# Turning k, q and scaled q of an mLSTM cell's second chunk by 128x128 transposes, with new hand-written orders

## The chip, the cores and the metric

One NeuronCore of one Trainium2 chip runs the whole kernel. The metric is device time in microseconds (us) for one execution. Below, PE is TensorE (PEld its weight loads), DVE is VectorE, ACT is ScalarE, POOL is GpSimd and SP is SyncE, which here only issues DMAs.

## The reference: an mLSTM cell, then a feed-forward block

Two blocks run one after the other. The first is a recurrent cell over 768 tokens, for 4 batches and 8 heads of 40 values each:

```python
for t in range(S):
    m_new = np.maximum(f_gate[:, :, t] + m, i_gate[:, :, t])
    f_stab = np.exp(f_gate[:, :, t] + m - m_new)
    i_stab = np.exp(i_gate[:, :, t] - m_new)
    C = f_stab * C + i_stab * outer(vt, kt)      # per batch and head, 40 x 40
    n = f_stab * n + i_stab * kt
    h = C @ qt;  denom = max(abs(n . qt), 1)
    y[:, :, t] = sigmoid(o_gate[:, :, t]) * h / denom
```

The second block takes the 3072 rows of 320 values and computes `leaky_relu(x @ w_in) @ w_out` with slope 0.01, where `w_in` is 320x2048 and `w_out` 2048x320. Everything is wanted in float32, but the two weight matrices arrive as float64.

## The kernel before

**Chunks, steps, groups.** The tokens are cut into six chunks of 128. A *step* is one chunk of one batch, with all 8 heads: steps 0 to 3 are chunk 0, steps 4 to 7 chunk 1, and so on. Inside a chunk the recurrence is done in closed form with matmuls (scores k.q, weights from exponents of gate sums, values, state). The outputs of the four steps of a chunk make one *group* of 512 rows for the feed-forward block. While the feed-forward of group g runs, the cell steps of chunk g+1 are put between its matmuls, and the times below fall into three parts: chunk 0 alone (0 to 38 us, "the front"), group 0 with chunk 1 beside it (38 to 129 us), and groups 1 to 5.

**Who sets the order.** PE, DVE, ACT and POOL run exactly in program order. For the front, that order is the string `ORDER` (line 1104): a list of small actions, each of which issues its instructions on its engines. The ones needed here: `ld`, `lo`, `lw`, `fd`, `ll` issue loads on SP (inputs, output gate, weights); `g`, `ge`, `ug` compute, exponentiate and turn the gates; `ab n` spreads gate sums over the partitions with matmuls (line 464) and `abw n` adds a mask to them on DVE (line 474); `tr s i` and `tc s i` turn k (i=0) or q (i=1) of step s on PE and copy the result on ACT (lines 581, 587); `sc` makes scores on PE, `exp` the weights on ACT (line 491), `scm` multiplies the two on DVE (line 603); `st` and `stc` make and copy the state; `val`, `den`, `gate` and `gp` make values, denominators, gated outputs and their scaling (PE, DVE, DVE, POOL); `x s` and `xc s` turn the outputs into `xT` (lines 879, 892); `vu`, `ps`, `tiles` prepare operands on POOL; `warm n` is n matmuls of the identity into a bank that nobody reads (line 338); and `ff j b0 b1` makes hidden columns j for batches b0 to b1.

**Narrowing.** The float64 weights are turned into float32 in seven passes for each of 12 pieces (lines 262 to 279): the first on ACT, six on DVE. `nw n` issues the next pass for piece n (`nw 0 0` and `nw 0 1` for the halves of piece 0). Pieces 0 to 3 are `w_in`, pieces 4 to 11 are `w_out`. From piece 2 on, the passes are dealt out during group 0 by the tuple `PASSES`.

**Group 0.** Its feed-forward is a list of 30 units. Units 0 and 1 are the last two batches of the first two hidden columns; units 2 to 13 are the rest of the hidden columns (line 910), piece 2 being needed from unit 6 and piece 3 from unit 10; units 14 to 29 are the second matmul (line 946), each a quarter of the sum for one batch: units 14 to 17 need pieces 4 and 5, 18 to 21 pieces 6 and 7, 22 to 25 pieces 8 and 9, and 26 to 29 pieces 10 and 11. `PASSES[i]` passes go ahead of unit i; `fetch` says ahead of which unit weights are loaded; `place` says after which units the parts of chunk 1's steps go, in the order parts 4, plain 4, parts 5, plain 5, parts 6, plain 6, the gates of chunk 2, parts 7, plain 7, and then the four `xT` turns.

**A step of chunk 1.** `ahead(s)` first calls `u_split(s)`: natural k and q (tokens on partitions, 8 heads of 40) are turned with 32 matmuls against a 64x64 piece of the identity, one for each head, each of k and q, and each half u of the tokens. A float32 matmul shows as two instructions, so 64 stand in the profile (line 567). ACT copies the two banks into `kqT` with four copies of 40x512 (line 573). `prep_qs(s)` scales q on POOL (line 520). `u_parts(s)` starts with `split_qs(s)`: the scaled q is turned in the same manner, 16 matmuls (32 instructions, line 553) and two ACT copies (line 555) into the rows of `mixed(s)` that its other halves leave free. Then the scores and the state product follow (tile `sd`, lines 653 and 658), for which DVE multiplies by the weights (line 663). `u_plain(s)` is tile `hN` (line 716), the denominator, and the gated output (line 727, POOL line 705). PSUM has two pools of four banks: `mm` for the feed-forward, `ab` and `warm`; `c` for the cell.

Of the kernel before, what the change touches and what calls it, by code (L numbers as in the profile page):

```python
# [22 lines left out]
def kernel(  # L23
# [26 lines left out]
    nc = tc.nc  # L50
# [89 lines left out]
    def mixed(s):  # L140

        n = s % 2
        return qn[:, 2 * n : 2 * n + 2]
# [9 lines left out]
    def prepare_tiles():  # L153

        for u in range(2):
            nc.gpsimd.tensor_copy(cm2[ts(u, SL)], cmask[ts(u, SL), ts(u, SL)])
        for t in rb_t:
            nc.gpsimd.memset(t[:, :, RL:], 0.0)

# [243 lines left out]

    def natural(s, i):

        t = rb_t[s % NR][:, i]
        return t[:, : H * D].rearrange("p (h d) -> p h d", d=D)
# [107 lines left out]
    def prep_qs(s):  # L515
# [3 lines left out]
        d["qs"] = wk.tile([P, Dm], F32, name="y")[:].rearrange("p (h d) -> p h d", d=D)  # L519
        nc.gpsimd.tensor_tensor(  # L520
            d["qs"], natural(s, 1), gT[c][:, 2, ts(b, H)].unsqueeze(2).to_broadcast([P, H, D]), op=ALU.mult,
# [25 lines left out]

    def split_qs(s):

        tq = [psc.tile([P, H, SL], F32, name=f"tq{u}", tag="c") for u in range(2)]  # L550
        for h in range(H):
            for u, toks, rows in subs(s):
                nc.tensor.matmul(tq[u][rows, h, :], lhsT=st[s]["qs"][toks, h], rhs=ident[toks, toks], start=True, stop=True)  # L553
        for u, toks, rows in subs(s):
            nc.scalar.copy(mixed(s)[rows, u], tq[u][rows])

    def u_split(s):
# [3 lines left out]
        src = (d["k"], natural(s, 1))  # L561
        bank = [psc.tile([P, H, SL], F32, name=f"tk{r}", tag="c") for r in range(2)]
        for h in range(H):
            for i in range(2):
                for u, toks, rows in subs(s):
                    out_rows = rows if i == 0 else slice(SL * u, SL * u + D)
                    nc.tensor.matmul(  # L567
                        bank[u][out_rows, h, :], lhsT=src[i][toks, h, :D], rhs=ident[toks, toks], start=True, stop=True,
                    )
        for i in range(2):  # L570
            for u, toks, rows in subs(s):
                out_rows = rows if i == 0 else slice(SL * u, SL * u + D)
                nc.scalar.copy(d["kqT"][rows, i].rearrange("p (h t) -> p h t", t=SL), bank[u][out_rows])
# [531 lines left out]
warm 2; warm 2; g 0; ld 1; ld 0; ge 0; lo 0; ld 2  # L1105
# [3 lines left out]
st 0; o 0; tc 1 1; exp 0; scm 0; exp 1; stc 0; st 1  # L1109
stc 1; warm 5; warm 1; sc 1; warm 6; scm 1; val 0; ab 2  # L1110
g 1; abw 2; abw 3; tr 2 0; tc 2 0; o 1; tr 2 1; val 1
warm 1; tr 3 0; vu 2; ps 1; ge 1; nw 0 0; den 0; gate 1
gate 0; tc 2 1; vu 3; tiles; tc 3 0; exp 2; o 2; warm 5
sc 2; gp 0; den 1; scm 2; nw 0 1; nw 0 0; nw 0 0; ug 1
warm 2; warm 1; nw 0 0; nw 0 1; x 0; tr 3 1; val 2; nw 0 1
warm 4; st 2; xc 0; tc 3 1; exp 3; gate 2; den 2; sc 3
stc 2; gp 1; scm 3; x 1; gp 2; ps 0; fd 4; nw 0 0
nw 0 0; nw 0 1; st 3; ll 4 1; lw 2; warm 5; val 3; nw 0 1
nw 0 0; xc 1; o 3; gate 3; den 3; nw 0 1; nw 0 1; nw 1
nw 1; stc 3; nw 1; ps 3; nw 1; ll 4 2; lw 3; x 2  # L1120
warm 1; ff 0 0 2; gp 3; ps 2; fd 5; ll 5 1; lw 4; x 3
xc 2; xc 3; lw 5; fd 6; fd 7; nw 1; nw 1; ff 1 0 2
ll 5 2; lw 6; nw 1
# [33 lines left out]
    with tc.manual_schedule(engines={E.PE, E.DVE, E.Activation, E.Pool}):  # L1157
        ffs = first_chunk()
        fetch = {1: (3, 4), 16: (7,), 12: (5, 6)}
        PASSES = (6, 0, 3, 0, 3, 3, 0, 3, 0, 2, 1, 0, 5, 1, 11, 0, 1, 3, 3, 3, 1, 12, 2, 3, 4, 0, 2, 1, 2, 21)  # L1160
        place = (1, 6, 11, 12, 16, 18, 19, 20, 22, 23, 25, 25, 26)
# [173 lines left out]
```

## Time and profile before

| what | value |
|---|---|
| median of 3 runs | 484.6 us (484.34 to 484.87) |
| profiled execution, its own time | 484.43 us |
| its span, first to last instruction | 482.3 us |
| around the span (484.43 - 482.3) | 2.1 us |
| PE busy in the span | 476.0 us, 99% |
| DVE, ACT, POOL busy in the span | 364.7, 196.1, 159.9 us |
| granted TensorE clock, mean | 1.000 |

Busy time says how long an engine had an instruction in it. In the stretch from 38 to 130 us, where the changed code lies, the two engines that matter are both nearly full, so neither the mean over the span nor one engine alone tells what a saved microsecond is worth: the order of each queue must be followed.

### The profile page before, as it was taken

The page shows a single profiled execution, that of the slowest core. Times are in us where ns is not written, and L with a number is a line of the kernel's source. Part 1 is how long each engine was busy: PE and PEld are TensorE (multiplying, and loading weights), DVE is VectorE, ACT ScalarE, POOL GpSimd, SP SyncE. Part 2 cuts the span into 40 slices and gives each one's busy share as a digit, 9 for nine tenths or more (in the row PEclk, how much of TensorE's full clock was granted, in tenths as well). Part 3 has the DMA queues.
Part 4 walks back from the last instruction along what each step waited for, and adds up shares of the span by engine and source line. Part 5 has one row for each costly group of instructions (what it writes and reads, how often), then busy time and mean ns, then how long its engine had stood idle before and what let it go on. Part 6 is the DMA issues. An engine that isn't in the chain of part 4 may idle for free.

```text
span 482.3 us, 12771 instructions
## 1 busy us (share of the span) xinstructions
PE 476.0 (99%) x5093; PEld 375.0 (78%) x5093; DVE 364.7 (76%) x601; ACT 196.1 (41%) x499; POOL 159.9 (33%) x207
## 2 busy tenths in 40 slices
PE   8999999999999999999999999999999999999997
PEld 7998855777655499955569985548998899988996
DVE  4689997989917989877897957889899967335611
ACT  3596774553732332305251212624025642156310
POOL 4146052452602727545641645462310002000020
PEclk9999999999999999999999999999999999999999
DMA  7877679786745577677787867773250030100001
GB/s 139 191 156 194 153 181 240 198 196 149 169 116 117 141 155 193 146 173 189 151 185 155 227 145 179 177 184 114 75 217 29 0 110 1 56 1 1 1 1 54
DMA packets 142698, 63.40 MB, mean 131 GB/s; under 512 B 110832, under 2 KB 130864, under 8 KB 142640
## 3 DMA queue, kind: packets, MB, share of 16 engines
q1 hardware_dynamic: 142256, 62.47, 53.8%
q8 instruction: 40, 0.66, 0.6%
q10 hardware_dynamic: 384, 0.13, 0.1%
q14 instruction: 18, 0.15, 0.1%
HBM read 51.68 MB, written 8.27 MB: 124 GB/s over the span
## 4 chain that ended last, share of the span: by engine, by line
PE 95%; DMA 1%; ACT 1%; DVE 1%; issue 0%; ACTq 0%; SPq 0%
PE po L985 32%; PE ph L910 29%; PE ph L836 8%; PE po L946 7%; PE pe L836 4%; PE pT L746 3%; PE sd L653 3%; PE warm L338 1%; PE sd L658 1%; PE hN L716 1%; PE tk L567 1%; PE tq L553 1%; DMA qn<-in_q_dram 1%; PE pa L676 1%; PE sc L596 1%; ACT w L491 0%
## 5 line engine op out<-in xcount | busy, mean ns | idle before, releaser
L910 PE MATMUL ph<-xT,w_in 64*128 64x512 f32 (+1 forms) x680 | 142.3, 569 | 0.4 <-DVE w_in L279 0.3
L910 PEld LDWEIGHTS ph<-xT,w_in 64*128 64x128 f32 x680 | 69.9, 187 | 61.8 <-issue 58.1
L985 PE MATMUL po<-w_out,acts 128*128 128x160 f32 x640 | 90.2, 300 | 0.0
L985 PEld LDWEIGHTS po<-w_out,acts 128*128 128x128 f32 x640 | 87.4, 190 | 1.9 <-ACT w L491 0.8
L918 ACT ACTIVATE acts<-ph 128x512 f32<-128x512 f32 (+1 forms) x68 | 35.1, 567 | 80.3 <-PE ph L910 80.1
L491 ACT ACTIVATE w<-w,gT 128x64 f32<-128x64 f32 (+1 forms) x192 | 51.7, 347 | 27.2 <-POOL w L483 27.2
L631 POOL TENSOR_TENSOR S<-S,f 40x336 f32<-40x336 f32 x36 | 34.2, 949 | 72.9 <-PE pT L746 50.5
L985 PE MATMUL po<-raw,acts 128*128 128x160 f32 x320 | 45.1, 299 | 0.0
L985 PEld LDWEIGHTS po<-raw,acts 128*128 128x128 f32 x320 | 44.0, 190 | 0.0
L1018 POOL TENSOR_TENSOR y<-y,raw 128x160 f32<-128x160 f32 x10 | 6.3, 634 | 113.4 <-ACT y L1017 113.4
L663 DVE TENSOR_TENSOR qn<-w,sd 64x512 f32<-64x512 f32 x40 | 27.4, 685 | 20.3 <-PE sd L658 14.2
L946 PE MATMUL po<-w_out,acts 128*128 128x320 f32 x128 | 36.6, 437 | 0.0
L483 POOL TENSOR_TENSOR w<-w,i 128x512 f32<-128x512 f32 x20 | 31.8, 1588 | 13.4 <-DVE late L264 13.3
L858 DVE SCALAR_TENSOR_TENSOR acts<-ph,acts 128x512 f32<-128x512 f32 x32 | 20.6, 685 | 20.6 <-ACT acts L856 20.6
L544 DVE TENSOR_TENSOR qn<-kqT,late 64x512 f32<-64x512 f32 x32 | 35.0, 1093 | 1.0
L946 PEld LDWEIGHTS po<-w_out,acts 128*128 128x128 f32 x128 | 23.6, 190 | 9.8 <-issue 0.8
L760 POOL TENSOR_TENSOR xb<-xb,den 128x320 f32<-128x320 f32 x16 | 11.6, 727 | 47.8 <-DVE xb L757 47.8
L856 ACT ACTIVATE acts<-pe 128x512 f32<-128x512 f32 x32 | 17.4, 594 | 19.0 <-PE pe L836 18.9
L653 PEld LDWEIGHTS sd<-kqT 40*64 40x64 f32 x640 | 20.1, 135 | 4.5 <-issue 4.3
L764 DVE STREAM_TRANSPOSE x<-xb 128x512 f32<-128x512 f32 x16 | 17.7, 1106 | 7.7 <-POOL xb L760 7.7
L862 ACT ACTIVATE acts<-acts 128x512 f32<-128x512 f32 x32 | 19.7, 633 | 8.1 <-DVE acts L858 8.1
L985 PE MATMUL po<-raw 128*128 128x160 f32 x160 | 22.8, 300 | 0.0
(166 smaller groups left out, 779.1 us busy)
## 6 DMA issues: line engine op xcount, KB each, us to landing
w<-a_dr SPq DMA_DIRECT2D x40, 128.0 KB, 3.5
rb<-in_k_dram SPq DMA_DIRECT2D x64, 80.0 KB, 3.3
rb<-in_q_dram SPq DMA_DIRECT2D x64, 80.0 KB, 2.6
rb<-in_o_gate_dram SPq DMA_DIRECT2D x64, 80.0 KB, 2.5
xT<-x_dr SPq DMA_DIRECT2D x32, 160.0 KB, 3.2
late<-a_dr SPq DMA_DIRECT2D x32, 128.0 KB, 3.4
x_dr<-x SPq DMA_DIRECT2D x16, 256.0 KB, 3.4
kn<-in_k_dram SPq DMA_DIRECT2D x24, 160.0 KB, 3.5
```

What stands on the lines that cost most here:

```text
L483: nc.gpsimd.tensor_tensor(w, w, cm2.unsqueeze(1).to_broadcast([P, H, SL]), op=ALU.add)
L491: yield nc.scalar.activation(w[:, h, :], w[:, h, :], AF.Exp, bias=gT[c][:, 0, bh : bh + 1], scale=1.0)
L544: nc.vector.tensor_tensor(mixed(s)[rows, 1 - r], d["kqT"][rows, 1].rearrange("p (h t) -> p h t", t=SL), d["ea"][rows], op=ALU.mult,)
L631: nc.gpsimd.tensor_tensor(new, old, g, op=ALU.mult)
L653: nc.tensor.matmul(bank[1 - u][toks, h, :], lhsT=kqT[rows, 0, ts(h, SL)], rhs=kqT[rows, 1, ts(h, SL)], start=True, stop=True,)
L663: nc.vector.tensor_tensor(mixed(s)[toks, u], w[toks], bank[1 - u][toks], op=ALU.mult)
L836: nc.tensor.matmul(ph[r][:], lhsT=parts["w", key][n][part, at : at + P], rhs=xs[key][part, slot, :], start=start and slot == 0, stop=stop ...
L858: nc.vector.scalar_tensor_tensor(fs[r], in0=ph[r][:], scalar=1.0 + EPS, in1=fs[r], op0=ALU.mult, op1=ALU.add,)
L910: nc.tensor.matmul(ph[r][:, cols], lhsT=w_row(r, slot, j), rhs=xT[DP * r : DP * (r + 1), slot, bs, :], start=(slot == 0), stop=(slot == KC ...
L918: nc.scalar.activation(acts[:, f, cols], ph[r][:, cols], AF.Prelu, alpha=0.01)
L946: nc.tensor.matmul(po[n][:], lhsT=acts[:, f, ts(n, P)], rhs=w_out[:, f, :], start=(f == 0), stop=(f == NF - 1),)
L985: nc.tensor.matmul(bank[:], lhsT=left[:, f, :], rhs=right[:, f, :], start=f == 0, stop=f == KH - 1)
```

## The change

1. *Chunk 1's turns.* `u_split` turns k and q with four transposes each, of 128 tokens by two heads of 64 (40 values and 24 of padding): 8 instructions for 64. `split_qs` does the same with the scaled q: 4 for 32. The banks then hold all 128 tokens of a head pair, so `to_halves` copies them out with four ACT copies of 40x256 for each bank: 8 copies for 4 in `u_split`, 4 for 2 in `split_qs`. The scaled q's turn takes one bank for two.
2. *Where q lies.* Natural q of chunk 1 is loaded with a stride of 64 a head; the padding is zeroed by two more POOL memsets in `tiles`. The scaled q goes into slot 0 of `mixed(s)` (tile `qn`) instead of a tile `y`.
3. *`ORDER`.* On PE: one `warm` fewer at the start, four more between `st 0` and `st 1`, one more between `ff 0` and `x 3`; `tr 2 1` goes behind `val 1`; `st 3` ahead of `x 1`; `ff 0 0 2` becomes `ff 0 0 1; ff 0 1 2`. On DVE: `stc 0` ahead of `scm 0`; `abw 3` ahead of `abw 2`; `scm 2` ahead of `den 1`; the fourth pass of `nw 0 1` ahead of `scm 3`; the third of `nw 1` ahead of `stc 3`. On POOL `ps 2` goes ahead of `gp 3`. On SP, the weights of `lw 4` and `lw 6` each go one load earlier.
4. *Group 0.* `place` puts parts 5 after unit 10 (11 before), plain 7 after unit 23 (22) and the third `xT` turn after unit 26 (25). `PASSES` moves single passes by one unit. `fetch` names other units for the late weights.

```diff
--- before.py
+++ after.py
@@ -156,6 +156,7 @@
             nc.gpsimd.tensor_copy(cm2[ts(u, SL)], cmask[ts(u, SL), ts(u, SL)])
         for t in rb_t:
             nc.gpsimd.memset(t[:, :, RL:], 0.0)
+            nc.gpsimd.memset(t[:, 1, : H * DP].rearrange("p (h d) -> p h d", d=DP)[:, :, D:], 0.0)
 
     def prepare_step(n):
 
@@ -401,8 +402,14 @@
             st[s]["o"].rearrange("p (h d) -> p h d", d=D), o_gate[b, :, ts(c, P), :].rearrange("h p d -> p h d"),
         )
 
+    def padded(s):
+
+        return rb_t[s % NR][:, 1, : H * DP].rearrange("p (h d) -> p h d", d=DP)
+
     def natural(s, i):
 
+        if i == 1:
+            return padded(s)[:, :, :D]
         t = rb_t[s % NR][:, i]
         return t[:, : H * D].rearrange("p (h d) -> p h d", d=D)
 
@@ -516,9 +523,8 @@
 
         c, b = divmod(s, B)
         d = st[s]
-        d["qs"] = wk.tile([P, Dm], F32, name="y")[:].rearrange("p (h d) -> p h d", d=D)
         nc.gpsimd.tensor_tensor(
-            d["qs"], natural(s, 1), gT[c][:, 2, ts(b, H)].unsqueeze(2).to_broadcast([P, H, D]), op=ALU.mult,
+            mixed(s)[:, 0, :, :D], natural(s, 1), gT[c][:, 2, ts(b, H)].unsqueeze(2).to_broadcast([P, H, D]), op=ALU.mult,
         )
 
     def prep_o(s):
@@ -545,32 +551,30 @@
                 mixed(s)[rows, 1 - r], d["kqT"][rows, 1].rearrange("p (h t) -> p h t", t=SL), d["ea"][rows], op=ALU.mult,
             )
 
+    def turned(name, src):
+
+        bank = psc.tile([P, PR, P], F32, name=name, tag="c")
+        for j in range(PR):
+            nc.tensor.transpose(bank[:, j, :], src[:, 2 * j : 2 * j + 2, :].rearrange("p h d -> p (h d)"), ident[:])
+        return bank
+
+    def to_halves(s, bank, dst):
+
+        for u, toks, rows in subs(s):
+            by = dst(u, rows).rearrange("p (j e) t -> p j e t", e=2)
+            for e in range(2):
+                nc.scalar.copy(by[:, :, e, :], bank[DP * e : DP * e + D, :, toks])
+
     def split_qs(s):
 
-        tq = [psc.tile([P, H, SL], F32, name=f"tq{u}", tag="c") for u in range(2)]
-        for h in range(H):
-            for u, toks, rows in subs(s):
-                nc.tensor.matmul(tq[u][rows, h, :], lhsT=st[s]["qs"][toks, h], rhs=ident[toks, toks], start=True, stop=True)
-        for u, toks, rows in subs(s):
-            nc.scalar.copy(mixed(s)[rows, u], tq[u][rows])
+        to_halves(s, turned("tq", mixed(s)[:, 0]), lambda u, rows: mixed(s)[rows, u])
 
     def u_split(s):
 
         d = st[s]
         d["kqT"] = cw.tile([P, 2, PR * P], F32, name="kqT")
-        src = (d["k"], natural(s, 1))
-        bank = [psc.tile([P, H, SL], F32, name=f"tk{r}", tag="c") for r in range(2)]
-        for h in range(H):
-            for i in range(2):
-                for u, toks, rows in subs(s):
-                    out_rows = rows if i == 0 else slice(SL * u, SL * u + D)
-                    nc.tensor.matmul(
-                        bank[u][out_rows, h, :], lhsT=src[i][toks, h, :D], rhs=ident[toks, toks], start=True, stop=True,
-                    )
-        for i in range(2):
-            for u, toks, rows in subs(s):
-                out_rows = rows if i == 0 else slice(SL * u, SL * u + D)
-                nc.scalar.copy(d["kqT"][rows, i].rearrange("p (h t) -> p h t", t=SL), bank[u][out_rows])
+        for i, bank in enumerate([turned("tk0", d["k"]), turned("tk1", padded(s))]):
+            to_halves(s, bank, lambda u, rows: d["kqT"][rows, i].rearrange("p (h t) -> p h t", t=SL))
 
     def u_transpose(s, i):
         d = st[s]
@@ -1102,25 +1106,25 @@
             nc.tensor.matmul(st["warm"][:], lhsT=ident[:], rhs=ident[:], start=True, stop=True)
 
     ORDER = """
-warm 2; warm 2; g 0; ld 1; ld 0; ge 0; lo 0; ld 2
+warm 2; warm 1; g 0; ld 1; ld 0; ge 0; lo 0; ld 2
 lw 0; lo 1; warm 6; warm 5; ab 0; ug 0; tr 1 0; tr 0 0
 tc 1 0; ld 3; lo 2; tr 0 1; abw 1; abw 0; warm 1; tc 0 1
 tc 0 0; tr 1 1; sc 0; warm 3; vu 1; vu 0; lw 1; lo 3
-st 0; o 0; tc 1 1; exp 0; scm 0; exp 1; stc 0; st 1
-stc 1; warm 5; warm 1; sc 1; warm 6; scm 1; val 0; ab 2
-g 1; abw 2; abw 3; tr 2 0; tc 2 0; o 1; tr 2 1; val 1
-warm 1; tr 3 0; vu 2; ps 1; ge 1; nw 0 0; den 0; gate 1
-gate 0; tc 2 1; vu 3; tiles; tc 3 0; exp 2; o 2; warm 5
-sc 2; gp 0; den 1; scm 2; nw 0 1; nw 0 0; nw 0 0; ug 1
-warm 2; warm 1; nw 0 0; nw 0 1; x 0; tr 3 1; val 2; nw 0 1
-warm 4; st 2; xc 0; tc 3 1; exp 3; gate 2; den 2; sc 3
-stc 2; gp 1; scm 3; x 1; gp 2; ps 0; fd 4; nw 0 0
-nw 0 0; nw 0 1; st 3; ll 4 1; lw 2; warm 5; val 3; nw 0 1
-nw 0 0; xc 1; o 3; gate 3; den 3; nw 0 1; nw 0 1; nw 1
-nw 1; stc 3; nw 1; ps 3; nw 1; ll 4 2; lw 3; x 2
-warm 1; ff 0 0 2; gp 3; ps 2; fd 5; ll 5 1; lw 4; x 3
-xc 2; xc 3; lw 5; fd 6; fd 7; nw 1; nw 1; ff 1 0 2
-ll 5 2; lw 6; nw 1
+st 0; o 0; tc 1 1; exp 0; stc 0; scm 0; exp 1; warm 4
+st 1; stc 1; warm 1; warm 5; sc 1; warm 6; scm 1; val 0
+ab 2; g 1; abw 3; abw 2; tr 2 0; tc 2 0; o 1; val 1
+warm 1; tr 2 1; tr 3 0; vu 2; ps 1; ge 1; nw 0 0; den 0
+gate 1; gate 0; tc 2 1; vu 3; tiles; tc 3 0; exp 2; o 2
+warm 5; sc 2; gp 0; scm 2; den 1; nw 0 1; nw 0 0; nw 0 0
+ug 1; warm 2; warm 1; nw 0 0; nw 0 1; x 0; tr 3 1; val 2
+nw 0 1; warm 4; st 2; xc 0; tc 3 1; exp 3; gate 2; den 2
+sc 3; stc 2; gp 1; nw 0 1; st 3; scm 3; x 1; gp 2
+ps 0; fd 4; nw 0 0; nw 0 0; ll 4 1; lw 2; warm 5; val 3
+nw 0 1; nw 0 0; xc 1; o 3; gate 3; den 3; nw 0 1; nw 0 1
+nw 1; nw 1; nw 1; ll 4 2; lw 3; x 2; warm 1; ff 0 0 1
+ff 0 1 2; ps 2; gp 3; fd 5; stc 3; nw 1; ps 3; warm 1
+lw 4; ll 5 1; x 3; xc 2; xc 3; lw 5; fd 6; fd 7
+nw 1; nw 1; ff 1 0 2; lw 6; nw 1; ll 5 2
 """
 
     def first_chunk():
@@ -1156,9 +1160,9 @@
     E = mybir.EngineType
     with tc.manual_schedule(engines={E.PE, E.DVE, E.Activation, E.Pool}):
         ffs = first_chunk()
-        fetch = {1: (3, 4), 16: (7,), 12: (5, 6)}
-        PASSES = (6, 0, 3, 0, 3, 3, 0, 3, 0, 2, 1, 0, 5, 1, 11, 0, 1, 3, 3, 3, 1, 12, 2, 3, 4, 0, 2, 1, 2, 21)
-        place = (1, 6, 11, 12, 16, 18, 19, 20, 22, 23, 25, 25, 26)
+        fetch = {1: (3, 4), 9: (5, 6), 17: (7,)}
+        PASSES = (6, 0, 3, 0, 3, 3, 0, 3, 0, 2, 1, 0, 5, 1, 11, 0, 1, 3, 3, 3, 2, 13, 1, 3, 3, 1, 2, 0, 1, 22)
+        place = (1, 6, 10, 12, 16, 18, 19, 20, 23, 23, 25, 26, 26)
         late = {}
         now = (None for n in range(2, QN + NF // 2) for _ in narrow_weights(n))
 
```

## The prediction

> **What bounds the kernel now.** The page comes first: the shares of the engines and the chain that ended last.
>
> ```profile
> PE 476.0 (99%) x5093; PEld 375.0 (78%) x5093; DVE 364.7 (76%) x601; ACT 196.1 (41%) x499; POOL 159.9 (33%) x207
> ...
> PE 95%; DMA 1%; ACT 1%; DVE 1%; issue 0%; ACTq 0%; SPq 0%
> ```
>
> PE is on the path for 95% of the span. But PE also counts as busy in `warm`, so the front needs its own look. I read the chain in order of time there and at the changed turns (start, length, what):
>
> ```profile
> 13.19 0.74 PE dC L611 x31
> 13.94 1.53 PE warm L338 x12
> ...
> 23.95 0.44 PE tkq L581 x4
> ...
> 37.97 2.43 PE ph L910 x20
> 40.40 0.37 PE xt L879 x2
> ...
> 43.43 1.03 PE tk L567 x64
> 44.46 4.52 PE ph L910 x40
> 48.98 1.02 PE tq L553 x32
> ```
>
> The reader is to see three prices: twelve warm instructions cost 1.53 us, four 128x128 transposes 0.44 us (0.11 each), and today's turns 1.03 us (`tk`) and 1.02 us (`tq`) a step. Next the timeline of DVE, with what ended its idle time:
>
> ```profile
> 21.01 0.28 DVE L303 TENSOR_TENSOR a<-F,m 32x128 f32<-32x128 f32 x1 [2.01 <-PE ab L464]
> ...
> 33.28 1.28 DVE L603 TENSOR_TENSOR w<-w,sc 128x512 f32<-128x512 f32 x2 [0.46 <-ACT w L491]
> ...
> 77.65 1.40 DVE L663 TENSOR_TENSOR qn<-w,sd 64x512 f32<-64x512 f32 x2 [2.14 <-PE sd L658]
> ...
> 107.75 1.40 DVE L663 TENSOR_TENSOR qn<-w,sd 64x512 f32<-64x512 f32 x2 [0.96 <-ACT w L491]
> ...
> 119.32 0.83 DVE L279 SCALAR_TENSOR_TENSOR w_out<-w_out,late 128x640 f32<-128x640 f32 x1
> ```
>
> From 21.0 us, when PE releases it after `ab 2`, DVE is almost never idle until the last narrowing ends at 120.15. Unit 26, which needs that piece, starts on PE at 120.51: 0.36 us of slack. Piece 2 ends at 59.44 for a unit 6 that starts at about 60.3 (12 instructions of 0.22 before 62.93), pieces 6 and 7 at 94.17 for a unit 18 at 95.13. So PE sets the time in group 0, with DVE under 1 us behind in three places. What shifts both at 38 us shifts the end; what only PE saves is worth something only if DVE comes along. From 130 us PE has no wait and nothing is changed.
>
> **The front.** (a) *Warm.* One `warm` less at the start makes PE early for q, for which it already waits 0.50 us at 9.35: nothing. Four more stand behind `st 0`, eight instructions of 1.53/12 = 0.1275: **+1.0**. PE has no gap from 11.17 to 20.91, where `ab 2` ends, so `ab 2` ends 1.0 later, and with it begins the DVE run of 21.01. No wait is there to cover it. Bounds: 0 to +1.3.
>
> (b) *DVE's order.* `den 1` (26.25 to 26.86, 0.6 us) today fills the time until `exp 2` on ACT releases `scm 2` at 27.14. ACT follows PE through `tr 2 1` and moves by the same 1.0, so `scm 2` starts at about 28.1; with `den 1` behind it, its time joins the run: **+0.6**. Against this, a narrowing pass (L268, 0.74 to 0.82) goes ahead of `scm 3` into the 0.46 us wait: **-0.46**. `stc 0` ahead of `scm 0` falls into 3.22 us in which DVE waits for ACT: nothing, and if ACT were early, 0.3. `abw 3` and `abw 2` cost the same in either order.
>
> (c) *POOL.* Two more memsets like those of L158 (2 in 0.46) come ahead of `gp 0`, which ends at about 28.3 instead of 28.1; `x 0` is due on PE at 29.2 after the shift: nothing, and 0.3 without it. The other swaps on POOL and SP pass work due microseconds later: q of step 5 is issued at 56.94 for a turn at 63.9. Later, `fetch` passes no SP instruction of a step, so the queue is the same.
>
> So the first `ph` starts 1.0 + 0.6 - 0.46 = **1.1 later**, at 39.1. (d) *`ff 0 0` split.* 20 instructions of 256 columns take 2.43; now 40 of 128. From below, half the time each: 0. From above, no cheaper each: +2.4. Nearest is `sc` (40 rows, 128 columns, 16 in 1.09 to 1.16, 0.07 each): 2.8, **+0.4**. (e) *`warm 1`* ahead of `x 3`: **+0.3**; two instructions took 0.30 at 9.96. Some may lie in the 0.3 that `x 3` waits for POOL.
>
> **Chunk 1.** The rows behind the prices, median in the middle (ns):
>
> ```profile
> L567 PE MATMUL tk<-ident,kn x128: 216/216/247, 43.4 to 99.3; 64*40 64x64 f32 x128
> ...
> L573 ACT COPY kqT<-tk x16: 577/580/582, 47.7 to 101.4; 40x512 f32<-40x512 f32 x16
> ```
>
> ```profile
> L581 PE MATMUL tkq<-ident,kn x16: 272/273/328, 7.8 to 24.1; 128*128 128x128 f32 x16
> ```
>
> (f) *`tk`.* 64 instructions overlap so far that they take 1.03; 8 transposes take 8 x 0.11 = 0.88: -0.15. But a transpose behind `ph` starts badly: the `xt` pair at 40.40 takes 0.37 instead of 0.22, and 0.11 passes before the next `ph`. Step 4 comes from `ph` and goes back: +0.1. Steps 5 and 6 come from `hN` and go to `ph`: -0.04 each; step 7 goes to `po`: -0.15. Sum **-0.1**, between -0.6 and +0.4.
>
> (g) *`tq`.* 1.02, 0.97, 0.96 and 1.02 become 0.44, plus 0.15 behind `ph` in steps 4 and 5 and 0.1 on the way into `sd`: **-1.5**, between -1.0 and -2.1.
>
> (h) *Waits in `sd`.* It takes 0.97 in steps 5 and 6 but 1.36 and 1.34 in steps 4 and 7: in step 4 the last `kqT` copy ends at 50.04, in step 7 POOL's `vu` at 106.10. PE is 1.8 later in step 4 and POOL, which follows DVE, 1 earlier in step 7: **-0.4 and -0.4**.
>
> (i) *ACT.* Six copies of 0.58 a step become twelve. The nearest row is L893, 64x256 in 0.37: 2.97 for `kqT` instead of 2.37, 1.5 for `mixed` instead of 1.18. ACT waits 2 to 4 us in this stretch for `tk` and `tq`, and the scores come four units after the turn: nothing on PE, except in step 4, where the shift of (a) covers it; without that, +0.4. In step 7 DVE waits for this, below. (j) POOL's scaled q goes to `qn`, whose readers of two steps ago (`hN`) ended before POOL's previous `x`: nothing.
>
> **Does DVE come along?** It starts 1.1 late, but parts 5 come one unit earlier (8 x 0.22 = 1.8), so its 2.14 wait at 77.65 goes: `sd 5` ends at 76.5, DVE is there at 76.6, 1.0 earlier than now. At 107.75 it is released by ACT, hence by `tq 7`: 105.45 + 1.5 + 0.6 = 107.55. One narrowing pass (0.33) has moved ahead of that wait, so the last piece ends at 120.15 - 0.15 - 0.33 = 119.67. PE's saving from 39 us on is 0.1 + 1.5 + 0.8 = 2.4, its loss before 1.1 + 0.4 + 0.3 = 1.8: 0.6 early, and 0.33 more at unit 26, because one `xt` turn now comes after it: 119.58. PE waits 0.1.
>
> The sum is 1.8 - 2.4 + 0.1 = -0.5, rounded **-0.6**: 484.43 - 0.6 = 483.8 on the profiled execution, which lies 0.2 below the median of 484.6.
>
> [...] The four transposes in 0.44 us show a cadence of 0.11 though one lasts 273 ns; the granted clock was 1.00 in both stretches of 10 us that hold the first sixteen. [...]
>
> **The rivals.** *The front loses nothing.* If the four `warm` lie in a wait that this order of the queues creates and DVE's swaps pay, (a) and (b) are 0 or the -0.46 alone. For it: today's `warm` runs end where an operand arrives (`sc 1` at 15.47, `scm 0` done at 15.3). Against it: nothing in front of `st 1` waits today. Step 4 then keeps its `kqT` wait (+0.4): -0.5 - 1.1 - 0.46 + 0.4 = -1.7, between -1.7 and -2.7 with the bounds of (f) and (g): 481.7 to 482.8.
>
> *Slower: DVE becomes the bound at unit 26.* If `sd 5` does not release DVE when it arrives, for instance behind ACT's longer copies, the 1.1 of the front stay in its run: the last piece ends at 120.15 + 1.1 - 0.33 = 120.9 against PE's 119.58, and PE waits 1.3: -0.6 + 1.3 = +0.7, 485.1. It decides as soon as DVE is over 0.5 late at 107. With a dear split (d) both are later still: to 486.5. For it: slack under 1 us in three places. Against it: the 2.14 wait to be won back.
>
> *Transposes one after the other.* If the cadence does not hold and each costs its 273 ns, 48 are 13.1 us for the 8.1 of today: +5.0, 489.4. Against it: every run of `xt` and `tkq` at 0.11. That the change does not do what it says has no place here: fewer instructions are certain, only their worth is not.
>
> **How the numbers follow.** The forecast of 483.8 has 0.38 (483.0 to 484.7); the first rival 0.33; the slower one 0.25; the last 0.04. About 0.2%, 1 us, is what a measurement of this kernel can tell from no change, so faster means below 483.6, slower above 485.6. Faster: 0.08 of the forecast and 0.33, **0.41**; same: 0.30 and 0.04 of the slower rival, **0.34**; slower: **0.25**. The range runs from 481.7 to 486.0; it leaves out the last rival and the far ends of the other two.
>
> **What would show it.** Right: `tk` as 8 instructions in 0.9 us and `tq` as 4 in 0.45 to 0.6; `ab 2` ending at 21.9 and the first `ph` at 39.1; no DVE wait of 2 us at `sd 5`; chunk 1's group ending about 0.6 before 129.46. Wrong: a first `ph` at or before 38 (first rival); PE idle ahead of unit 6, 18 or 26, released by L279 (slower); a dip of the granted clock or a `tk` near 2 us (last).

## The result and the profile after

The changed kernel takes 486.54 us (median of 7 executions, 485.53 to 487.03) beside 484.87 of the kernel before on the same chip: a ratio of 1.0032, with a 95% interval of 1.0019 to 1.0045. A second set of 12 executions (e8, below) gave 486.25 and 1.0020 [1.0008, 1.0031]. The change costs 1.2 to 1.7 us. The forecast was 483.8, the upper end of the range 486.0; the sign of the forecast was wrong, and the time lies above the range. The profiled execution took 486.97, with a span of 485.1 (before: 484.43 and 482.3); it lies near the upper end of its seven. Two executions far outside the rest, 988.06 of e9 and 611.85 of the kernel before, are left out of the ratios as slow.

The page of the changed kernel, the lines that answer to those of before:

```profile
PE 477.9 (99%) x4785; PEld 374.9 (77%) x4785; DVE 365.1 (75%) x601; ACT 199.8 (41%) x525; POOL 160.1 (33%) x209
...
PEclk9998999999999999999999999999999999999999
...
PE 81%; DVE 10%; DMA 4%; issue 2%; POOL 2%; SPq 1%; ACT 0%; DVEq 0%; POOLq 0%
```

PE has 308 instructions fewer and is busy 1.9 us *longer*. The chain that ended last now runs through DVE for 10% and through DMA for 4% of the span, where it was 95% PE. And the granted clock has a dip in the fourth of forty slices. The first place is the front. The chain in order of time, the same steps as before (line numbers have moved by 1 to 9):

```profile
13.75 1.09 PE warm L339 x8
...
24.77 0.46 PE warm L339 x2
25.23 0.87 PE tkq L585 x8
...
36.07 1.29 DVE w L607 x2
37.35 0.68 DVE w_in L274
...
39.27 0.82 DVE w_in L280
...
40.13 4.13 PE ph L914 x40
...
47.37 1.03 PE tk L558 x8
...
52.91 0.59 PE tq L558 x4
```

The first `ph` starts at 40.13 (before: 37.97), released by DVE's last pass on `w_in` as before, and its 40 instructions take 4.13 where 20 took 2.43. The turn of step 4 starts at 47.37, 3.94 later than before. `tk` still takes 1.03 with 8 instructions for 64; `tq` takes 0.59 instead of 1.02. Four lines of DVE's timeline, the first from the kernel before and the others from the changed one:

```profile
27.14 1.28 DVE L603 TENSOR_TENSOR w<-w,sc 128x512 f32<-128x512 f32 x2 [0.28 <-ACT w L491]
...
22.35 0.28 DVE L304 TENSOR_TENSOR a<-F,m 32x128 f32<-32x128 f32 x1 [2.11 <-PE ab L471]
...
28.87 1.28 DVE L607 TENSOR_TENSOR w<-w,sc 128x512 f32<-128x512 f32 x2 [1.13 <-ACT w L498]
...
78.84 1.40 DVE L667 TENSOR_TENSOR qn<-w,sd 64x512 f32<-64x512 f32 x2 [1.51 <-ACT qn L566]
```

The DVE run starts 1.34 late, `scm 2` 1.73 late and after a wait of 1.13 (before: 0.28). At `sd 5` DVE still waits, now for ACT's copy of the turned q. Why `ff 0 0` took 4.13 is in a table of stretches (us from the start; length, busy PE; then granted clock, DMA share, GB/s):

```profile
36.00:40.00 4.00, 3.59 (x31) 1.00 0.86 204
40.00:40.50 0.50, 0.36 (x4) 0.88 0.90 270
40.50:43.50 3.00, 3.00 (x32) 0.50 0.68 204
43.50:44.00 0.50, 0.50 (x11) 0.71 0.74 180
44.00:48.00 4.00, 4.00 (x37) 1.00 0.86 222
```

Together the rows make 3.4 us at half clock. The second place lies where the prediction looked no further, from 350 us on. DVE's and PE's timeline there in the kernel before:

```profile
347.72 0.82 DVE L798 TENSOR_SCALAR tmp<-w_in 128x640 uint32<-128x640 uint32 x1
...
362.98 1.32 PE L836 MATMUL ph<-x_low,w_low 64*128 64x512 f32 x10
```

DVE's timeline, SP's waits and PE's timeline in the changed kernel:

```profile
351.26 0.49 DVE L802 TENSOR_SCALAR tmp<-w_in 128x640 uint32<-128x640 uint32 x1 [1.84 <-DMA x_dr<-x]
```

```profile
SPq L807 <- DMA x_dr<-x: 3.9, 1, 3.9
```

```profile
365.49 1.43 PE L840 MATMUL ph<-x_low,w_low 64*128 64x512 f32 x10 [0.61 <-ACT x_low L828]
```

The last of the transfers that carry chunk 5's outputs to DRAM (`x_dr<-x`, line 769) lands 4.3 us after its issue, where it took 2.3 before; SP waits 3.9 for it, 1.8 before. DVE's next work and SP's next load (`w_raw`, line 807) wait for it, ACT's `x_low` follows, and PE, with nothing to spare there, loses time.

The lag behind the kernel before, mark by mark: 2.16 at the first `ph`, 3.94 at the turn of step 4, 1.20 at the start of group 1 (130.59 for 129.39), 1.55 at 250 us, 1.60 at 361 us, 2.62 at 364 us, 2.87 from 390 us on, 2.8 in the span. So the front lost 3.9, the middle won back 2.7, 0.35 went between 130 and 250 us, and 1.3 from 362 to 390 us, 1.0 of it in the first three microseconds.

### The profile page after: what moved, and what is told of

It is laid out like the page before. It is cut to its first block, busy times and chain, and to the rows that moved or that the text cites. A ratio compares the mean times of both kernels' runs of the same rounds, so it can differ in the third digit from the quotient of the medians.

```text
span 485.1 us, 12182 instructions
## 1 busy us (share of the span) xinstructions
PE 477.9 (99%) x4785; PEld 374.9 (77%) x4785; DVE 365.1 (75%) x601; ACT 199.8 (41%) x525; POOL 160.1 (33%) x209
## 4 chain that ended last, share of the span: by engine, by line
PE 81%; DVE 10%; DMA 4%; issue 2%; POOL 2%; SPq 1%; ACT 0%; DVEq 0%; POOLq 0%
PE po L989 25%; PE ph L914 22%; PE ph L840 8%; PE po L950 7%; PE pe L840 4%; PE warm L339 3%; PE sd L657 2%; PE pT L750 2%; DMA x_dr<-x 1%; DVE qn L667 1%; PE sc L600 1%; DVE qn L550 1%; PE hN L720 1%; PE sd L662 1%; PE tk L558 1%
## 5 line engine op out<-in xcount | busy, mean ns | idle before, releaser
L914 PE MATMUL ph<-xT,w_in 64*128 64x512 f32 (+2 forms) x700 | 143.9, 564 | 0.4 <-DVE w_in L280 0.4
L922 ACT ACTIVATE acts<-ph 128x512 f32<-128x512 f32 (+2 forms) x70 | 35.3, 556 | 80.7 <-PE ph L914 80.6
L840 PE MATMUL ph<-x_low,w_low 64*128 64x512 f32 x160 | 22.5, 391 | 0.6 <-ACT x_low L828 0.6
```

The costliest lines, as they stand in the source:

```text
L840: nc.tensor.matmul(ph[r][:], lhsT=parts["w", key][n][part, at : at + P], rhs=xs[key][part, slot, :], start=start and slot == 0, stop=stop ...
L914: nc.tensor.matmul(ph[r][:, cols], lhsT=w_row(r, slot, j), rhs=xT[DP * r : DP * (r + 1), slot, bs, :], start=(slot == 0), stop=(slot == KC ...
L922: nc.scalar.activation(acts[:, f, cols], ph[r][:, cols], AF.Prelu, alpha=0.01)
```

## The experiments

Twelve kernels, each in five rounds; times are medians in us (number of executions), ratios are to the kernel before, run beside them (484.87 for e1 to e4, 485.02 for e5 to e8, 484.84 for e9 to e12).

| run | what | time | ratio [95%] |
|---|---|---|---|
| e1 | turns alone, old order and old group 0 | 484.30 (11) | 0.9986 [0.9977, 0.9994] |
| e2 | new front order alone, old turns | 487.34 (6) | 1.0053 [1.0041, 1.0065] |
| e3 | turns and new group 0, old front order | 482.62 (5) | 0.9957 [0.9945, 0.9970] |
| e4 | changed kernel without its four `warm` | 483.28 (5) | 0.9969 [0.9958, 0.9981] |
| e5 | e3 with the four `warm` | 483.19 (6) | 0.9968 [0.9956, 0.9979] |
| e6 | e3 with a pass ahead of `scm 3` | 482.30 (12) | 0.9955 [0.9942, 0.9968] |
| e7 | e6 without `warm 6` | 481.68 (5) | 0.9937 [0.9925, 0.9949] |
| e8 | changed kernel again | 486.25 (12) | 1.0020 [1.0008, 1.0031] |
| e9 | six `warm` in halves | 487.03 (11) | 1.0035 [1.0023, 1.0047] |
| e10 | ten `warm` in halves | 488.09 (6) | 1.0062 [1.0047, 1.0076] |
| e11 | `den 1` back ahead of `scm 2` | 485.20 (11) | 1.0002 [0.9992, 1.0011] |
| e12 | `ff 0 0` in one piece | 485.18 (12) | 1.0004 [0.9992, 1.0016] |

**e1, the turns alone.** The changed code with the order, `PASSES`, `fetch` and `place` of before:

```diff
-        fetch = {1: (3, 4), 9: (5, 6), 17: (7,)}
+        fetch = {1: (3, 4), 16: (7,), 12: (5, 6)}
...
-        place = (1, 6, 10, 12, 16, 18, 19, 20, 23, 23, 25, 26, 26)
+        place = (1, 6, 11, 12, 16, 18, 19, 20, 22, 23, 25, 25, 26)
```

> The changed turns (transposes, padded q, eight and four copies on ACT) with the old ORDER, PASSES, fetch and place. Theory F (the new order of the front loses about 4 us before the first turn and the turns win 2.7 back): the front is that of before, first ph near 38.0, and group 0 ends about 1.5 to 2.5 us earlier than at 129.46, so the time is 1 to 2.5 us below before (about 0.9955 of it). Rival T (the turns themselves cost, through the longer copies on ACT and the narrowing on DVE that then holds PE): no faster than before, PE idle ahead of unit 6, 18 or 26. Rival L (the loss arises late, where PE waits for ACT x_low near 363 us): the time does not follow the end of group 0.

Measured: 484.30, a gain of 0.6 where PE alone saves over 2. What took the rest stands in the waits of group 0:

```profile
PE tg L346 <- DVE hn L731: 0.7, 1, 0.7
PE sd L662 <- POOL vu L518: 0.5, 1, 0.5
```

The faster PE arrives before DVE and POOL and waits 1.2 us. What the turns save is worth little until the other queues are moved too.

**e2, the front order alone.** The kernel before, with the new `ORDER` string and nothing else.

> The kernel before with the new ORDER alone, nothing else changed. Theory F: first ph at about 40 instead of 38, step 4's turn about 3 to 4 us later than at 43.43, and nothing wins it back, so the end of group 0 comes 3 to 4 us later and the time is 487.5 to 489 us (1.006 to 1.009). Rival T: the front is harmless and the time stays within 1 us of before. Rival L: the front is later but the end of the span is 2 us later or less.

Measured: 487.34, 2.5 above before. Its profile has the same dip of the clock (`ff 0 0` takes 4.13 from 40.13 on), yet its executions with the clock at 1.000 are no better than 486.31 to 487.04: the new front loses without the dip as well.

**e3, turns and group 0.** The changed kernel with the old `ORDER`.

> The changed turns with the new PASSES, fetch and place, and the old ORDER. Theory F: as the turns alone, or 0.5 us better because DVE's wait of 2.14 us at sd 5 goes: 1.5 to 3 us below before. Rival T: no faster than before. Rival L: group 0 ends earlier but the time is not 1.5 us better.

Measured: 482.62, 2.25 below before. Group 1 starts at 127.33. With e1 and e2 this places the loss: the turns together with their group 0 gain, and the order of the front loses more than they gain.

**e4, without the four `warm`.**

```diff
-st 0; o 0; tc 1 1; exp 0; stc 0; scm 0; exp 1; warm 4
+st 0; o 0; tc 1 1; exp 0; stc 0; scm 0; exp 1
```

> The changed kernel without the four warm between st 0 and st 1. Theory F with the warm as its largest term: ab 2 ends at about 21.2 instead of 22.2, the first ph comes 1.0 us earlier than in the changed kernel, and the time is about 1 us lower, near that of before. If the warm only fill a wait, ab 2 and the first ph stay where they are and the time is that of the changed kernel (1.003).

Measured: 483.28, that is 3.0 to 3.3 below the changed kernel, for eight PE instructions that take 1.09. First `ph` at 38.55, the split `ff 0 0` in 2.50, the clock at 1.00 throughout, and the last `x_dr<-x` in 2.3. So `warm` cost its own length, and two things of more size appeared with it: the dip and the late transfer.

**e5, the four `warm` in the old order.**

```diff
-st 0; o 0; tc 1 1; exp 0; scm 0; exp 1; stc 0; st 1
+st 0; o 0; tc 1 1; exp 0; scm 0; exp 1; stc 0; warm 4; st 1
```

> The kernel of the turns with the new group 0 and the old ORDER (482.62 us), plus the four warm between st 0 and st 1 alone. If the four warm cost what they take on PE, ab 2 and the first ph come 1.0 us later (first ph near 38.7) and the time is 483.6, some of it perhaps recovered. If they cost the 3.2 us that taking them out of the changed kernel gave, the time is near 485.8, and a drop of the granted clock near 40 us, or a longer last x_dr transfer near 347 us, shows where the other 2 us go. If the clock drops only when the four meet the rest of the new order, there is no drop here and the time is 483.6.

Measured: 483.19, 0.6 above e3, although the front is late by 2.1 (first `ph` at 39.77 for 37.66, of which 0.9 is the start of the execution): group 0 gives back 0.7 of it. No dip, no late transfer. The four `warm` alone are cheap.

**e6, a pass into the wait at `scm 3`.** e3, with the fourth pass of `nw 0 1` ahead of `scm 3`, as in the changed kernel:

```diff
-stc 2; gp 1; scm 3; x 1; gp 2; ps 0; fd 4; nw 0 0
-nw 0 0; nw 0 1; st 3; ll 4 1; lw 2; warm 5; val 3; nw 0 1
+stc 2; gp 1; nw 0 1; scm 3; x 1; gp 2; ps 0; fd 4; nw 0 0
+nw 0 0; st 3; ll 4 1; lw 2; warm 5; val 3; nw 0 1
```

> The kernel of the turns with the new group 0 and the old ORDER, with the fourth pass of nw 0 1 ahead of scm 3 as in the new order. By the step of the prediction this fills DVE's wait of 0.46 us: the first ph comes 0.46 us earlier than with the old order and the time is about 482.2. If ACT's exp 3 is not what ends that wait, nothing changes (482.6).

Measured: 482.30, 0.3 below e3, inside both intervals. DVE's wait of 0.47 at `scm 3` is gone, as the step of the prediction had it. From DVE's `a` behind `ab 2` to the first `ph` it is 16.65 for e3's 16.96, so 0.3 of the 0.46 arrives, and in the time it is worth 0.3 at most.

**e7, without `warm 6`.** e6, and:

```diff
-stc 1; warm 5; warm 1; sc 1; warm 6; scm 1; val 0; ab 2
+stc 1; warm 5; warm 1; sc 1; scm 1; val 0; ab 2
```

> As the kernel with the pass ahead of scm 3, and the six warm between sc 1 and val 0 left out too. Theory: PE's warm ahead of ab 2 are on the path, because DVE's long run starts when ab 2 ends (it waits 2.0 us there). Then ab 2 ends 1.5 us earlier, the first ph comes 1 to 1.5 us earlier, and the time is about 481. Rival: the granted clock drops once PE idles, or DVE then waits for ACT instead: first ph unchanged or later, time 482 or more.

Measured: 481.68, 0.9937 [0.9925, 0.9949]: the fastest of all, ahead of both kernels. Only 0.6 below e6: counted from `ab 0`, DVE's run begins 1.3 earlier (12.74 for 14.08), and its wait for `ab 2` is 0.76 instead of 2.10, but from there to the first `ph` it takes 17.17 for 16.65, with a wait of 0.58 for `exp 2` at `scm 2` where e6 has 0.29. The mean clock was 1.000 in the profiled execution: the rival's drop did not come.

**e8, the changed kernel again.**

> The changed kernel once more, for a second profile. If the drop of the granted clock at 40.1 to 43.7 us and the last x_dr transfer of 4.3 us belong to the kernel, both are there again. If they are chance of one execution, ff 0 0 takes 2.5 us instead of 4.1 and the transfer 2.4 us, and the span is 2 us or more below 485.1; a time near 486.5 without them would mean that the loss of 3.2 us by the four warm lies elsewhere.

Measured: 486.25, and a profile with the same marks: `ff 0 0` in 4.13 from 40.31, SP's wait for `x_dr` 3.9, PE's wait for `x_low` 0.61. The clock was at 0.996 in the profiled execution and 0.999 to 1.000 in the other eleven (484.69 to 487.54). So the late transfer is no accident of one execution, and the dip alone does not explain the time.

**What the late transfer is.** The records of single packets say more than the views. In the changed kernel the 512 packets of the last `x_dr<-x` run from 347.74; fifteen of its sixteen completion records (4 bytes) are written by 348.77, the sixteenth at 350.69, behind 20 packets that come after all the others. One other packet lies there: 16,384 bytes of the queue named "instruction", from 348.19 to 349.86. In e8 it is the same (347.83, and 348.36 to 350.03). The page's row of that queue:

```profile
q8 instruction: 38, 0.62, 0.5%
```

and the window 346 to 352 of the changed kernel, in 40 slices:

```profile
GB/s 0 0 0 0 0 0 0 0 0 0 0 68 297 280 396 276 276 185 10 0 0 0 0 0 0 3 10 10 7 14 20 3 0 0 0 0 0 0 0 0
...
q8 instruction: 1, 0.02, 1.7%
...
x_dr<-x SPq DMA_DIRECT2D x1, 256.0 KB, 4.3
```

The bulk is over in eight slices; then a thin tail of 3 to 20 GB/s, and only behind it the 4.3 us. My reading, an estimate from these times and the sixteen completion records, since the records name no engine: a fetch of program code takes one of sixteen DMA engines for 1.67 us, and that engine's share of `x_dr` waits behind it; the 20 late packets begin at 349.85, as the code packet ends. There are 40 code packets with PE's 5093 instructions in the kernel before and 38 with 4785 in the changed one. That what PE executes before 350 us sets *when* the packet comes is an estimate from these counts and from one pair of runs: from e6 to e7, with 12 PE instructions fewer, it came 2.5 later against the work around it (5.65 and 8.12 after the burst's start). In the fourteen profiles this burst takes 1.02 to 1.04 us, but for three: both of the changed kernel and e11 below, and in these three a code packet begins inside it (in e4 one begins at its end, without effect). The next runs move it.

**e9, twelve more PE instructions over the same columns.**

```diff
-st 1; stc 1; warm 1; warm 5; sc 1; warm 6; scm 1; val 0
+st 1; stc 1; wh 1; wh 5; sc 1; warm 6; scm 1; val 0
...
+            for at in (slice(0, SL), slice(SL, P)):
+                nc.tensor.matmul(t[:, at], lhsT=ident[:], rhs=ident[:, at], start=True, stop=True)
```

> The changed kernel, but the warm 1 and warm 5 behind st 1 are issued as 12 matmuls of 64 columns instead of 6 of 128: 12 more PE instructions over the same columns. It tests why the last x_dr<-x takes 4.3 us in both profiles of the changed kernel and 2.3 elsewhere. Theory (a transfer of code in the way): in both of those profiles one packet of the instruction queue q8, of 16 KB, starts at 348.2 to 348.4, 0.45 to 0.53 us into the burst of 512 packets of that x_dr (347.74 on), and takes 1.68 us; fifteen of the sixteen completion records of x_dr are written by 348.76 and the last only at 350.7, when the engine that carried the code has written its last 20 packets. The count of q8 packets goes with PE's instructions (40 for 5093, 38 for 4785), and from e6 to e7, with 12 PE instructions fewer, this packet came 2.4 later. So 12 more bring it about 2.4 earlier, to about 345.8, ahead of the burst: SP's wait for x_dr is 1.8 to 1.9 again instead of 3.9, PE's wait for x_low at 365 is gone, and the time falls by 0.5 to 1.3 if the 64-column matmuls cost half of the 128-column ones (at the same price each the front loses up to 1.5 and the time stays). Rival (the late transfer comes with the later front, not with the code): SP still waits 3.9 us wherever the q8 packet lies, and the time does not fall.

Measured in the profile: the packet comes at 345.93 (forecast 345.8), before the burst of 347.64 to 348.66, which takes 1.02 again. The same window:

```profile
GB/s 0 0 0 0 0 0 0 0 0 0 10 246 297 290 290 290 266 58 0 0 0 0 0 0 0 0 0 0 171 375 478 410 375 375 512 375 444 307 512 376
...
x_dr<-x SPq DMA_DIRECT2D x1, 256.0 KB, 2.3
```

No tail, 2.3 us, and PE's wait for `x_low` is gone, although the front is later than in the changed kernel (first `ph` at 41.04: halves cost as much each as whole ones, 24 in 2.82 for 12 in 1.54). So lateness of the front does not make the transfer late. By the expectation the time then stays where it was, because the halves cost the front what the transfer no longer does. What was measured is less clear: 485.60 in the profiled execution, but 487.03 in the median, with values in two clusters, 485.6 to 485.9 and 486.7 to 487.5. What parts the clusters, with the clock at 0.999 to 1.000 in all, no record shows.

**e10, twenty more.** As e9, and `warm 4` becomes `wh 4`.

> As e9, with the warm 4 issued as 8 matmuls of 64 columns too: 20 more PE instructions than the changed kernel. Theory (code in the way): the q8 packet comes about 4.1 earlier than in the changed kernel, near 344.1, so it may fall into the burst of the x_dr before the last one (344.08 to 345.11) and not into the last: SP's wait for the last x_dr 1.8 to 2.2, no wait of 0.5 for x_low on PE, time 0.5 to 1.3 below the changed kernel if the halves cost half, about equal to it or 1 above if they cost the same each. Rival (later front): SP still waits 3.9 us.

Measured: the packet starts 2.4 ahead of the burst (347.86 and 350.24), not 4 as I had it, and clear of both bursts (the one before it ends at 347.6); SP's wait is 1.8. The price of the halves, 16 in 1.93 and 24 in 2.82, puts the first `ph` at 42.59, and the time at 488.09: the front's lateness counts, code or no code.

**e11, `den 1` back.**

```diff
-warm 5; sc 2; gp 0; scm 2; den 1; nw 0 1; nw 0 0; nw 0 0
+warm 5; sc 2; gp 0; den 1; scm 2; nw 0 1; nw 0 0; nw 0 0
```

> The changed kernel with den 1 back ahead of scm 2 on DVE, as before. The prediction's term (b) holds that den 1 then runs while DVE waits for exp 2, and that its 0.6 us leave the run: the first ph 0.5 to 0.6 earlier than in the changed kernel, and, since DVE is not late after parts 5, 0.3 to 0.6 in the time (485.7 to 486.2 beside 486.4). Rival: PE waits there for something else (scm 2 was put ahead because it is due first), so scm 2 starts 0.3 to 0.6 later than in the changed kernel, PE waits for it in val 2, and the first ph and the time do not move or move the other way by up to 0.6. Either way the position of the code packet is the same, so SP's wait for x_dr should stay near 3.9 unless the shift of the front moves the burst by more than 0.5 against it.

Measured: `scm 2` starts 6.55 after the end of `ab 2` as before the edit, and the pass behind it 0.51 earlier (7.75 for 8.26). DVE's line shows `den 1` back inside the wait:

```profile
29.11 1.28 DVE L607 TENSOR_TENSOR w<-w,sc 128x512 f32<-128x512 f32 x2 [0.64 <-ACT w L498]
```

1.13 has become 0.64. The first `ph` comes at 39.58. From DVE's `a` to the first `ph` it is 17.00 for 17.79 in the changed kernel: 0.79, more than `den 1` alone, since a narrowing pass (L267) that took 0.78 behind `scm 2` takes 0.36 again. The time falls by 1.1 to 1.3, more than the 0.3 to 0.6 expected; the profile has no dip, and a code packet that begins 0.92 into the burst and stretches it to 2.41 instead of 2.94 (SP waits 3.4). In e4 a packet began as far into the burst and left no tail; the records don't name DMA engines, so whether it had one that was done is open.

**e12, `ff 0 0` in one piece.**

```diff
-nw 1; nw 1; nw 1; ll 4 2; lw 3; x 2; warm 1; ff 0 0 1
-ff 0 1 2; ps 2; gp 3; fd 5; stc 3; nw 1; ps 3; warm 1
+nw 1; nw 1; nw 1; ll 4 2; lw 3; x 2; warm 1; ff 0 0 2
+ ps 2; gp 3; fd 5; stc 3; nw 1; ps 3; warm 1
```

> The changed kernel with ff 0 0 in one piece (20 instructions of 256 columns) as before. The prediction's term (d) gave the split +0.4; the undisturbed split of e4 took 2.50 for 2.43, so 0.1 is expected of it now, if the granted clock stays at 1.00. 20 PE instructions fewer move the q8 packet about 4 later, past the burst of the last x_dr: by the theory of the code in the way SP waits 1.8 to 1.9 for x_dr, PE does not wait for x_low, and the time falls by 0.5 to 1.3, to 485.1 to 485.9. Rival (the late transfer comes with the later front): SP's wait stays at 3.9. On the drop of the clock at 40 us, seen in three first executions of this order: if the 40 short instructions bring it, it is gone here; if the short waits of PE at 30 to 40 us do, it may show again at the same place.

Measured: the packet comes at 349.16, 2.8 after the start of a burst that takes 1.03; PE waits not at all for `x_low`, and SP as in the kernel before:

```profile
SPq L807 <- DMA x_dr<-x: 1.8, 1, 1.8
```

The time falls by 1.1 to 1.4, to 485.18. Both halves of the theory's forecast hold, though the split is undone here too, which is worth 0.07 without a dip (e4). The clock was at 0.996 in 4 of the 12 executions (485.73 to 485.90, beside a median of 484.5 for the others): the split is not what brings the dip, and a dip goes with about 1.3 in the time here. In group 0, PE now waits once, at unit 6, which the prediction gave as a sign of its slower rival (e9 and e11 have the same wait, 0.4):

```profile
PE ph L914 <- DVE w_in L280: 0.3, 1, 0.3
```

## Why the prediction was wrong, step by step

**The first step that failed is the front's sum, "its loss before 1.1 + 0.4 + 0.3 = 1.8".** It measured 3.94 in the profile. Of that 1.6 is the dip, which the mean clock shows in 3 of the 19 executions of the changed kernel. Without it the front loses 2.3 by the rows below, and the term that was mis-sized is (b): 0.6 - 0.46 = 0.14 forecast, 0.82 measured. Term by term:

- (a), four `warm` at +1.0: 1.22. They take 1.09 and cut a run of `dC` that took 0.74 into two of 0.44. From `ab 0` to DVE's `a` it is 15.30 in the six profiles with the four and no halves (the changed kernel, e2, e5, e8, e11, e12) and 14.08 without the four (e1, e3, e4, e6). DVE's run started 1.34 late; the other 0.12 is what was left of the very start, where `ab 0` began at 7.05 for 6.55. That mark moves from one execution to the next: e3 and e6, the same program up to there, have it at 6.61 and 7.79, since the 16 `warm` instructions from 4.6 us on take 2.07 in one and 3.24 in the other. So one profile cannot carry a term below a microsecond that is counted from its start; count from a mark inside it. The claim that no wait covers the `warm` was right; e5 shows that group 0 gives part of it back.
- (b), from DVE's `a` to the first `ph`: 16.96 in the profiles with the old order (before, e1, e3, e5), 17.78 to 17.80 in those with the new one (the changed kernel, e2, e4, e8, e9, e10, e12), so **+0.82**. `den 1` at +0.6: 0.51 at the pass behind `scm 2`, 0.79 at the first `ph` (e11), as one pass takes 0.78 for 0.36 with it. The pass into the wait before `scm 3`, at -0.46: the wait is gone, 0.31 of it arrives (e6). And the step had ACT "move by the same 1.0" and priced the move of `tr 2 1` behind `val 1` at nothing. There it stands behind `warm 1`, which waits 0.22 for DVE's `w` of `abw` (L481), and `exp 2` begins 1.72 late instead of 1.34: **0.39** that the sum lacked. It is in the runs with that order (from DVE's `a` to `scm 2` 6.52 in the changed kernel and in e4, 6.13 before and in e5). No run moves `tr 2 1` alone, so this cause is read from the queues and not shown by an edit.
- (d), the split at +0.4. Undisturbed it costs 0.07 (2.50 for 2.43, e4), less than forecast. In the profiled execution the clock halved and it cost 1.70. Of the last rival, "a dip of the granted clock" was named as a sign; it came, but not from the new transposes, which lie behind it: it is in e2, which has none in the turns. (e), `warm 1`: 0.15 for 0.3.

**The middle was right.** (f) saved the 0.1 forecast: 1.02 in steps 4 to 6 and 0.93 in step 7, for 1.03 each. The transposes follow each other at 0.109 in a group of eight as in one of four; the rest is 0.165 ahead of the second and 0.20 between the last and the next `ph`. (g) and (h) together, from the start of each `tq` to the end of its `sd`, went from 8.64 to 6.38 over four steps: 2.26 saved, forecast 1.5 + 0.8. (i) held at 0.366 a copy. From the first turn to group 1 the changed kernel saves 2.74 and e9, e11 and e12 save 2.0 with a PE wait of 0.3 to 0.4 in it, beside 2.4 forecast.

Two slips in the sum decide nothing: -0.5 is "rounded" to -0.6, and DVE's release at 107.55 instead of 107.75 enters as 0.15.

**DVE's slack was misread, without harm here.** The forecast had DVE released at `sd 5` on arrival; instead it waits 1.51 for ACT's copy of the turned q, the very condition of the slower rival. Its last piece ended at 121.61, not 119.67. PE did not wait, because it was late too, and because unit 26, which began at 121.21, evidently did not need the piece's last pass at its first matmul, as I had assumed. In e1 that rival is real: 1.2 us of PE waits.

**The second failure is a sentence: "From 130 us PE has no wait and nothing is changed."** Nothing was edited there, yet the lag grew by 1.7: by 0.35 up to 250 us (in e3, e9, e11 and e12 as well, not in e4; the cause is open) and by 1.3 from 362 us on. In an execution without the dip this is the larger part of the miss. By my reading of the packets, the changed count of PE's instructions (4785 for 5093) moved the points at which code is fetched, and in this program one fetch (348.19 to 349.86) fell into a transfer (from 347.74) on which the start of the last groups hangs. In e9 and e12 the packet lies ahead of the burst and behind it (345.93 and 349.16), and the delay is gone: behind 361 us their lag does not grow at all, and in e11, with the shorter stretch, it grows by 1.0. In the median time, e12 alone shows it; e9 pays for the halves.

Put together from the times: turns with their group 0 -2.25 (e3 against before), the new front order in one piece +2.56 (e12 against e3), the split with the dip and the place of the code packet +1.1 to +1.4 (changed kernel against e12), in all +1.4 to +1.7. The three are differences along one chain of kernels and so add up to what was measured in any case. How the last of them divides in executions without a profile is open, and so is what brings the dip: it stands in both profiles of the changed kernel and in that of e2, not in those of e9 to e12 with the same four `warm`, and the mean clock of single executions of e6, e12 and the kernel before points to one there too. In all three it begins about 0.2 to 0.4 after the first `ph` does (40.38 for 40.13 in the changed kernel). PE waits only 0.15 to 0.40 at a time in the ten microseconds ahead of it (busy 9.59 of 10), and it is busy 2.87 of the last 3.42, a stretch as long as the dip; from 9.66 to 13.07 it is busy 2.74 of 3.41 in the same profile, and no dip follows there. A drop behind an idle PE shows at the end of the changed kernel: PE's last work ends at 481.54, and the clock is 1.00 from 482 to 484 and 0.55 from 484 to 485. No idle stretch of that length, 2.5 us, stands before the dip.

## What to carry to other kernels

A saving on the bounding engine is worth its length only if the queues beside it come along: the turns alone gave 0.6 of over 2 us, with the schedule moved 2.25. When an order is changed, price every item that is moved, also a turn that slides behind a filler, and test each edit of a searched order by itself: here most of the new front cost time, and the old one with the new turns, one pass moved and `warm 6` left out (e7) is 3.3 us faster than the kernel before. After a change in the count of instructions, look at the whole timeline, not at the edited part: here a landing time at 350 us, with every edit before 130, went from 2.3 to 4.3 us, with a code packet inside the burst.

## What the runs showed of the hardware

A code packet of 16,384 bytes took 0.9 to 1.8 us, 40 times in the profile of the kernel before and 38 times in that of the changed one; the last `x_dr<-x`, 256 KB, lands in 2.3 us where its burst takes 1.02, and in 4.3 (both profiles of the changed kernel) or 3.9 (e11) where such a packet begins inside the burst, though in e4, where one begins 0.92 into it, it lands in 2.3. The packet's place against the burst moved in the runs that change PE's instruction count, not in proportion to it: 2.2 earlier for 12 more (e9), 2.8 for 20 more (e10), 2.4 later for 20 fewer (e12), 2.5 for 12 fewer (e7 against e6), 0.5 for 8 fewer (e4) and 0.5 with none changed (e11). Float32 128x128 transposes follow each other at 0.109 us in a group of four or eight, with 0.165 ahead of the second and 0.20 behind the last where the group stands between `ph`. A float32 matmul of the identity against 64 columns took nearly as long as one against 128 (e9: 24 instructions in 2.82 for 12 in 1.54). The granted clock fell to half for 3.4 us in the profile of the changed kernel, although PE waited at most 0.40 at a time in the ten microseconds before it; in e12 the executions with a mean clock of 0.996 are 1.3 us longer, and single ones of e6 and of the kernel before 3.1 and 2.4 above their medians, while 3.4 us at half clock take at most 1.7 of PE's work, an estimate from the length.
